# A planned transformer block on one core: the planner's durations are replaced by measured ones, and its settings and random draws are chosen again

## The chip, the cores and the metric

The kernel runs on one NeuronCore of a Trainium2 chip. The metric is the device time of one execution in microseconds (us). Five engines work side by side, each through its own instructions in a fixed order: PE (TensorE, matrix products), DVE (VectorE), ACT (ScalarE), POOL (GpSimd) and SP (SyncE, which here only issues transfers). They wait for each other through semaphores.

## The reference

One block of attention and one of an MLP, each behind a layer norm, over 2048 rows of 512 numbers, all in float32:

```python
h  = x + A(layernorm(x), wqkv, wo)
h2 = h + B(layernorm(h), w1, b1, w2, b2)

def A(x, wqkv, wo):          # 32 heads of 16; 8 keys a row, every second row back from it
    q, k, v = split(x @ wqkv)
    idx = pos[:, None] - 2 * arange(8)[None, :]
    logits = where(idx >= 0, einsum("hsd,hswd->hsw", q, k[idx]) * 16 ** -0.5, -1e9)
    return einsum("hsw,hswd->hsd", softmax(logits), v[idx]) @ wo

def B(x, w1, b1, w2, b2):    # 512 -> 1792 -> 512
    return relu(x @ w1 + b1) ** 2 @ w2 + b2
```

## The kernel before

**Products.** Every operand of a product is split into a high and a low part of a rounded float32 type (`hi` on ACT is a cast, `lo` on POOL or DVE a subtraction), and a product runs in three passes on PE: high by high, high by low and low by high. A pass over 128 rows and 512 columns is four matmuls of 512 columns.

**Groups.** The 2048 rows are worked in four groups of 512 (`u` = 0 to 3 in the code, four tiles of 128 rows each). For all groups x is normed, turned on PE and multiplied by `wqkv` (`qkv_first`, `qkv`); y goes to memory (`qkv_d`). The attention of a group is four items (`item`, one for 8 heads, so 16 in all). An item loads k, q and v; ACT copies q to PSUM (`qp`); DVE forms two products `pr<-qp,k` and sums them (`le<-pr`), does the softmax in small steps (ACT does the exponential, `le<-le`), forms two products `pr<-le,v`; POOL adds each of these up in three steps (`pr<-pr` of 1024, `pr<-pr` of 512, `o<-pr` of 256 numbers a row). There are three `pr` buffers.

**From attention to MLP** (`to_mlp`). For group 0 PE turns o (`tr<-ident,o`). For the other groups o is written to memory (`o_d<-o`, four times), read back in another order (`back<-o_d`), turned in blocks on DVE (`turned<-back`) and split by `split_turned`, whose operands have a stride: ACT casts `oh<-turned`, POOL subtracts `ol<-turned,oh`. Then PE multiplies by wo (`wo<-`), DVE adds h (`h<-wo,h`), and h is normed. For group 0 that is BN_STATS and BN_AGGR on DVE, three small operations on POOL (`rs`), the norm on ACT (`hn<-h,rs`) and a turn on PE (`tr<-ident,hn`). For the others it is four passes and a norm on ACT (`norm_act`), a way through memory (`t_d`, `back<-t_d`), `turned<-back` on DVE and the strided cast `big_h<-turned`. The result lies in `big_h` and `big_l`, in the place of the previous group's, so the casts wait until PE has read that for the last time.

**MLP.** For each of 14 blocks f of 128 hidden columns: PE multiplies by w1 (`mm<-`; for the first six blocks the weights are `w1a_h` and `w1a_l`, so the first matmul of a group's MLP reads `mm<-big_h,w1a_h`), ACT does the ReLU and the square (`r`, L742 and L744), ACT casts `rh<-r`, POOL subtracts `rl<-r,rh`, and PE adds the product with w2 to four sums (`acc<-w2s,rh` twice, `acc<-w2s,rl` once). The last group does pairs of blocks by a Winograd scheme (`win_pair`, `win_weights`, `win_rows`). w2 is split once (`w2_job`), kept in memory (`w_d`) and loaded again for every group (`w2s<-w_d`).

**What sets the order.** The code first records all work as tasks with a duration on each engine that may do it (`plan.add`); then `deadlines` gives each a due time, counted back from PE's place, with a random part (`NOISE`, `SEEDS`: one seed for each 40 us), and `schedule` places them one after another: on each engine the task that can start first, among equals the one due first. Some tasks may go to POOL or DVE, and the planner decides (`lo`, `add_any`). The instructions are then written out in the planned order; so the durations decide only about order and engine, and the chip waits where the order doesn't fit.

Durations come from `dv(n)` (DVE), `ac(n)` (ACT), `po(n)` (POOL) for n numbers a row, from numbers in the calls, and from `dma_us`. Settings are `BEFORE` (how much earlier the items of each group are due), `W2_EACH` (distance of the due times of `w2_job`), `LEAD` (how much earlier PE's turns rank), `NOISE` and `SEEDS`.

Of the kernel before, what the change touches and what calls it, by code (L numbers as in the profile page):

```python
# [15 lines left out]
S, D, H, DH, W, F = 2048, 512, 32, 16, 8, 1792  # L16
# [16 lines left out]
FA = 6  # L33
WARM = 46
ITEM = 16.0
BEFORE = 8, 16, 4, 16
X_BY_DRAM = (14, 15)
W2_EACH = 4.5
LO = ("POOL",)
LAGW = 2  # L40
NOISE, SEEDS = 0.3, (
    487, 765, 735, 246, 644, 701, 83, 442, 213, 893, 112, 220, 567, 914)
WIN = (0, 1, 2, 3, 4, 5, 6)
LEAD = 6.0
BY_PE = (0,)
TO_MLP = 10
T0 = 8.0
# [192 lines left out]


def dv(n):
    return (n + 157) / 960 + 0.01


def ac(n):
# [1 line left out]


def po(n):  # L250
    return 0.25 + 0.00214 * n


def dma_us(count, packet):
# [4 lines left out]
def block_kernel(ctx, tc, x, wqkv, wo, w1, b1, w2, b2, out):  # L259
    nc = tc.nc  # L260
# [47 lines left out]
    plan = Plan(bufs)  # L308
# [11 lines left out]
    def act(n, fn, extra=0.0, **k):  # L320
        return plan.add({"ACT": ac(n) + extra}, lambda e: fn(), **k)

    def vec(n, fn, **k):
        return plan.add({"DVE": dv(n)}, lambda e: fn(), **k)

    def pool(us, fn, **k):
        return plan.add({"POOL": us}, lambda e: fn(), **k)
# [2 lines left out]
        return plan.add({"SP": 0.45 if plan.pe < T0 + 1 else 0.55}, lambda e: fn(nc.sync),  # L330
                        dma=dma_us(count, packet), **k)

    def hi(n, dst, src, r, w, **k):
        act(n, lambda: nc.scalar.copy(dst(), src()), r=r, w=w, **k)  # L334

    def lo(n, dst, src, h, r, w, engs=("POOL", "DVE"), port=True, **k):
        cost = {"POOL": po(n), "DVE": dv(n)}
        plan.add({e: cost[e] for e in engs},
                 lambda e: engines[e].tensor_tensor(out=dst(), in0=src(), in1=h(),  # L339
                                                    op=ALU.subtract), r=r, w=w, port=port, **k)  # L340
# [18 lines left out]
    def norm_vec(src, dst, delay):  # L359
        st, mv, rs = (buf(n, (P, k)) for n, k in (("st", 6), ("mv", 2), ("rs", 2)))  # L360
        plan.add({"DVE": 0.70}, lambda e: nc.vector.bn_stats(st.get(), src.get()), r=[src], w=[st])
        plan.add({"DVE": 0.20}, lambda e: nc.vector.bn_aggr(mv.get(), st.get()), r=[st], w=[mv])

        def scale(e):
            m, s = mv.get(), rs.get()
            nc.gpsimd.tensor_scalar(out=s[:, 1:2], in0=m[:, 1:2], scalar1=EPS, scalar2=None,
                                    op0=ALU.add)
            nc.gpsimd.tensor_tensor(out=s[:, 0:1], in0=s[:, 1:2], in1=mhalf, op=ALU.pow)
            if delay:
                nc.gpsimd.tensor_scalar(out=s[:, 1:2], in0=m[:, 0:1], scalar1=s[:, 0:1],  # L370
                                        scalar2=-1.0, op0=ALU.mult, op1=ALU.mult)
        plan.add({"POOL": 1.15 if delay else 0.85}, scale, r=[mv, "mhalf"], w=[rs])
        if delay:
            act(D, lambda: nc.scalar.activation(blocked(dst, True), natural(src, True), AF.Identity,
                                                scale=rs.get()[:, 0:1], bias=rs.get()[:, 1:2]),
                0.2, r=[src, rs], w=[dst])
        else:

            plan.add({"DVE": 0.57}, lambda e: nc.vector.tensor_scalar(
                out=dst.get(), in0=src.get(), scalar1=mv.get()[:, 0:1], scalar2=None,  # L380
                op0=ALU.subtract), r=[src, mv], w=[dst])
        return rs

    def norm_act(src, dst, cls, by_pe):

        sq, sv = row("sq", cls), buf("sv", (P, 4))

        def sums(e):
            s = sv.get()
            nc.scalar.activation(sq.get(), src.get(), AF.Copy, accum_out=s[:, 0:1])  # L390
            nc.scalar.activation(s[:, 1:2], s[:, 0:1], AF.Copy, scale=-1.0 / D)
            nc.scalar.activation(sq.get(), src.get(), AF.Square, bias=s[:, 1:2],
                                 accum_out=s[:, 2:3])
            nc.scalar.activation(s[:, 3:4], s[:, 2:3], AF.Copy, scale=1.0 / D, bias=EPS)  # L394
        plan.add({"ACT": 2.2}, sums, r=[src], w=[sv, sq])
        pool(0.6, lambda: nc.gpsimd.tensor_tensor(out=sv.get()[:, 0:1], in0=sv.get()[:, 3:4],  # L396
                                                  in1=mhalf, op=ALU.pow), r=["mhalf"], w=[sv])

        def apply(e):
            s = sv.get()  # L400
            nc.scalar.activation(s[:, 2:3], s[:, 1:2], AF.Copy, scale=s[:, 0:1])
            nc.scalar.activation(blocked(dst, by_pe), natural(src, by_pe), AF.Identity, scale=s[:, 0:1],
                                 bias=s[:, 2:3])
        plan.add({"ACT": 1.1}, apply, r=[src, sv], w=[dst, sv])


    def pe_turn(srcs, r, **k):
# [49 lines left out]

    def split_turned(t, name):
        h, l = [row(name + p, CLASS[name], (P, KB, P), F32R) for p in "hl"]
        hi(D, lambda: by_block(h.get()), lambda: by_row(t), r=[t], w=[h])  # L460
        lo(D, lambda: by_block(l.get()), lambda: by_row(t), lambda: by_block(h.get()),
           r=[t, h], w=[l], engs=LO)
        return h, l

    def mm(n, ps, terms, width, start, stop, r, **k):
# [97 lines left out]
    def item(u, g, due, o):  # L563
        b, e = divmod(u, 2)
        src = lambda c: [("S", c, g, t) for v in ((u, u - 2) if b else (u,))
                         for t in range(v * R, v * R + R)] + ["zero"]
# [4 lines left out]
        def win(c, dst):  # L571
# [7 lines left out]
            r=src(0), w=[q], by=due - 8)  # L579
# [5 lines left out]
        for n, i0 in enumerate((0, IQ)):  # L585
# [5 lines left out]
                r=[qp, ks], w=[pr], by=due + 5 * n)  # L591
# [3 lines left out]
                r=[pr], w=[(LE, i0)], by=due + 5 * n + 1)  # L595
        if u < 2:
            tt("DVE", 256, lg, lg, lambda: mask.unsqueeze(3).to_broadcast([P, R, W, GH]), ALU.add,
               r=["mask"], w=lgs, by=due + 6)
        mx, sm = buf("mx", (P, R, GH)), buf("sm", (P, R, GH))
        vec(300, lambda: nc.vector.tensor_reduce(  # L600
            out=mx.get(), in_=lg().rearrange("p i w h -> p i h w"), axis=X, op=ALU.max),
            r=lgs, w=[mx], by=due + 6)
        tt("DVE", 256, lg, lg, lambda: mx.get().unsqueeze(2).to_broadcast([P, R, W, GH]),
# [1 line left out]
        act(256, lambda: nc.scalar.activation(LE.get()[:, 1], LE.get()[:, 0], AF.Exp,  # L605
                                             scale=DH ** -0.5),
            r=lgs, w=[exs], by=due + 6)
        vec(300, lambda: nc.vector.tensor_reduce(
            out=sm.get(), in_=ex().rearrange("p i w h -> p i h w"), axis=X, op=ALU.add),
            r=[exs], w=[sm], by=due + 8)  # L610
        vec(64, lambda: nc.vector.reciprocal(sm.get(), sm.get()), w=[sm], by=due + 8)
        tt("DVE", 256, ex, ex, lambda: sm.get().unsqueeze(2).to_broadcast([P, R, W, GH]),
           ALU.mult, r=[sm], w=[exs], by=due + 8)
        own = o is None
# [66 lines left out]
    def wo_product(t, oh, ol, h, pe, **k):  # L681
        ps = buf("ps", (P, D), name="wo")
        mm3(ps, ps.get, D, oh, ol, (lambda k: wo_h[:, k, :], [("wo", 0, k) for k in range(KB)]),
            (lambda k: wo_l[:, k, :], [("wo", 1, k) for k in range(KB)]), **k)
        tt("DVE", D, h.get, ps.get, h.get, ALU.add, r=[ps], w=[h], by=k["first"] + 3)
        hn = row("hn", "B")
        if pe:
            norm_vec(h, hn, True)
        else:
            norm_act(h, hn, "B", False)  # L690
        i = t % R
        if pe:
            ht = pe_turn([block(hn, k) for k in range(KB)], [hn])
        else:
            ht = turned(hn, "B")
        keys = [B(p, range(KB), [i]) for p in range(2)]

        def parts():
            if pe:
                view, src = lambda p: hh(p)[:, :, i, :], ht.get  # L700
            else:
                view, src = lambda p: by_block(hh(p)[:, :, i, :]), lambda: by_row(ht)
            hi(D, lambda: view(0), src, r=[ht], w=keys[0])
            lo(D, lambda: view(1), src, lambda: view(0), r=[ht] + keys[0],
               w=keys[1], engs=("DVE",) if pe else ("POOL", "DVE"), port=not pe)
# [47 lines left out]
    TT = [buf("pr", (P, 4, D), F32R, "tt") for _ in range(2)]  # L753

    def add_any(n, out_, a, b, op, **k):
        plan.add({"POOL": po(n), "DVE": dv(n)},
                 lambda e: engines[e].tensor_tensor(out=out_(), in0=a(), in1=b(), op=op),
                 port=True, **k)

# [176 lines left out]
    def consts():  # L936
# [1 line left out]
        nc.gpsimd.memset(mask, 0.0)  # L938
        nc.gpsimd.affine_select(out=mask, in_=mask, pattern=[[1, R], [1, W]], base=1 - W,
                                channel_multiplier=R, compare_op=ALU.is_ge, fill=NEG)  # L940
    pool(0.6, consts, w=["zero_sb", "mask"], by=0.0)
    load(192, 512, lambda q: q.dma_start(
        chain(0, 0, 0, 0, [[GC, PAD], [CS, 6 * G], [1, GC]]),
        zero.unsqueeze(1).to_broadcast([PAD, 6 * G, GC])), r=["zero_sb"],
# [207 lines left out]
```

## Time and profile before

| | us |
|---|---|
| median of 3 runs (lowest, highest) | 520.13 (519.19, 520.32) |
| the profiled execution, its own time | 520.07 |
| its span in the profile | 518.3 |
| PE busy | 502.3 |
| DVE busy | 369.3 |
| POOL busy | 334.0 |
| ACT busy | 302.1 |

The profile is one execution. A row of the timeline names the start, the length, the engine, the line, the operation and the tiles as out<-in; in brackets stands how long the engine had been idle before it, and what ended that. Matmuls overlap: a row of four matmuls of 512 columns lasts 1.07 us, but the next starts 0.91 us after it began. Idle time of an engine is a loss only where the end hangs on it.

### The profile page before, as it was taken

Reading aid. Unit: us, or ns where it says so; the run is one execution under the profiler, and the core shown is the slowest. Engines: PE = TensorE matmul, PEld = TensorE weight load, DVE = VectorE, ACT = ScalarE, POOL = GpSimd, SP = SyncE. Lnnn points to the kernel's source line nnn. Section 1 sums busy time; section 2 is a strip of 40 time slices with the busy share of each in tenths; the row PEclk is TensorE's granted clock in tenths of the full one; section 3 lists DMA queues with packets and bytes.
Section 4 is the critical chain, followed back from the end, with each engine's and each line's share of the span. In section 5 each row is a group of like instructions: output and inputs, shape, how many; then the busy total and the mean of one; then the engine's idle time right before and its main releaser. Section 6 shows DMA issues by size and latency. Waiting matters only on the chain.

```text
span 518.3 us, 7193 instructions
## 1 busy us (share of the span) xinstructions
PE 502.3 (97%) x2426; PEld 423.8 (82%) x2426; DVE 369.3 (71%) x406; ACT 302.1 (58%) x582; POOL 334.0 (64%) x282
## 2 busy tenths in 40 slices
PE   8999999999997999899989999999999999999997
PEld 8998888888876887687778888778887887988885
DVE  6379989989869877996774889988012486765633
ACT  4549868686254532579653467755356956574341
POOL 6102888784879697699889468679835132378920
PEclk9999999999998999999999999999999999999999
DMA  8699599999979975968784865934462856799842
GB/s 255 185 306 281 199 291 324 367 408 395 335 270 311 335 259 153 352 211 287 255 310 148 301 230 196 345 130 163 162 225 83 243 190 211 268 312 345 278 144 81
DMA packets 90229, 131.43 MB, mean 254 GB/s; under 512 B 7504, under 2 KB 57168, under 8 KB 90192
## 3 DMA queue, kind: packets, MB, share of 16 engines
q1 hardware_dynamic: 90048, 130.84, 75.2%
q8 instruction: 19, 0.31, 0.3%
q14 instruction: 18, 0.15, 0.1%
q10 hardware_dynamic: 144, 0.13, 0.1%
HBM read 93.63 MB, written 37.36 MB: 253 GB/s over the span
## 4 chain that ended last, share of the span: by engine, by line
PE 40%; POOL 11%; issue 6%; ACT 5%; DMA 5%; DVE 5%; SPq 1%; POOLq 0%; ACTq 0%; DVEq 0%
PE acc L880 17%; PE mm L469 11%; PE mm L840 6%; PE wo L469 4%; POOL pr L637 4%; DMA raw<-in_B_w_dram 2%; DVE pr L587 2%; ACT big_h L334 2%; DMA back<-o_d 2%; DMA back<-t_d 1%; POOL rl L339 1%; POOL o L637 1%; POOL ol L339 1%; POOL w2s L339 1%; DVE le L592 1%
## 5 line engine op out<-in xcount | busy, mean ns | idle before, releaser
L637 POOL TENSOR_TENSOR pr<-pr 128x1024 f32<-128x1024 f32 (+1 forms) x64 | 117.4, 1848 | 7.3 <-DVE pr L619 6.8
L880 PE MATMUL acc<-w2s,rh 128*128 128x512 f32 x444 | 111.4, 390 | 1.7 <-ACT rh L334 1.7
L339 POOL TENSOR_TENSOR rl<-r,rh 128x512 fp32r<-128x512 f32 x48 | 63.2, 1317 | 60.8 <-ACT rh L334 50.4
L880 PEld LDWEIGHTS acc<-w2s,rh 128*128 128x128 f32 x444 | 82.5, 188 | 19.1 <-ACT rh L334 2.5
L587 DVE TENSOR_TENSOR pr<-qp,k 128x2048 f32<-128x2048 f32 x32 | 72.6, 2278 | 17.1 <-POOL o L637 13.1
L619 DVE TENSOR_TENSOR pr<-le,v 128x2048 f32<-128x2048 f32 x32 | 72.6, 2285 | 11.6 <-POOL o L637 11.0
L592 DVE TENSOR_REDUCE le<-pr 128x128 f32<-128x2048 f32 x32 | 72.9, 2278 | 0.6
L742 ACT ACTIVATE r<-mm,b_sb 128x512 f32<-128x512 f32 x42 | 28.8, 686 | 72.0 <-PE mm L469 68.3
L880 PE MATMUL acc<-w2s,rl 128*128 128x512 f32 x222 | 60.5, 390 | 0.0
L469 PE MATMUL mm<-big_h,xh 128*128 128x512 f32 (+1 forms) x208 | 49.5, 376 | 0.3 <-ACT xh L334 0.3
L469 PE MATMUL mm<-big_h,xl 128*128 128x512 f32 (+1 forms) x208 | 49.7, 375 | 0.0
L469 PE MATMUL mm<-big_l,xh 128*128 128x512 f32 (+1 forms) x208 | 49.0, 374 | 0.0
L880 PEld LDWEIGHTS acc<-w2s,rl 128*128 128x128 f32 x222 | 41.0, 188 | 7.9
L469 PEld LDWEIGHTS mm<-big_h,xh 128*128 128x128 f32 x208 | 37.7, 188 | 6.3 <-ACT xh L334 1.1
L469 PEld LDWEIGHTS mm<-big_l,xh 128*128 128x128 f32 x208 | 38.1, 188 | 5.6
L469 PEld LDWEIGHTS mm<-big_h,xl 128*128 128x128 f32 x208 | 37.9, 188 | 5.4
L440 DVE STREAM_TRANSPOSE turned<-back 128x512 f32<-128x512 f32 x26 | 17.7, 696 | 28.9 <-DMA back<-o_d 19.6
L334 ACT CAST rh<-r 128x512 fp32r<-128x512 f32 x56 | 34.5, 619 | 1.6
L546 ACT COPY y<-mm 128x512 f32<-128x512 f32 x36 | 20.7, 587 | 14.9 <-PE mm L469 9.6
L469 PE MATMUL mm<-big_h 128*128 128x512 f32 x96 | 25.9, 394 | 2.1 <-ACT r L742 2.1
L744 ACT ACTIVATE r<-r 128x512 f32<-128x512 f32 x42 | 26.6, 634 | 1.0
L396 POOL TENSOR_TENSOR sv<-sv,mhalf 128x1 f32<-128x1 f32 x24 | 13.1, 549 | 21.7 <-ACT sv L394 21.6
(157 smaller groups left out, 956.6 us busy)
## 6 DMA issues: line engine op xcount, KB each, us to landing
w2s<-w_d SPq DMA_DIRECT2D x56, 512.0 KB, 4.7
k<-qkv_d SPq DMA_DIRECT2D x16, 704.0 KB, 5.5
v<-qkv_d SPq DMA_DIRECT2D x16, 704.0 KB, 4.9
raw<-in_B_w_dram SPq DMA_DIRECT2D x42, 256.0 KB, 6.6
qkv_d<-y SPq DMA_DIRECT2D x18, 512.0 KB, 6.6
w_d<-w2s SPq DMA_DIRECT2D x14, 512.0 KB, 6.5
xt<-in_A_x_dram SPq DMA_DIRECT2D x16, 256.0 KB, 4.3
q<-qkv_d SPq DMA_DIRECT2D x16, 256.0 KB, 6.6
```

Of the source, the lines that this page charges most:

```text
L334: act(n, lambda: nc.scalar.copy(dst(), src()), r=r, w=w, **k)
L339: lambda e: engines[e].tensor_tensor(out=dst(), in0=src(), in1=h(), op=ALU.subtract), r=r, w=w, port=port, **k)
L469: nc.tensor.matmul(ps(), l(), rr(), start=start and i == 0, stop=stop and i == len(terms) - 1)
L546: act(D, lambda: nc.scalar.copy(y.get()[:, :, j, :], ps.get().rearrange("p (j c) -> p j c", c=GC)), r=[ps], w=[(y, j)], by=plan.pe + 3)
L587: vec(2048, lambda pr=pr, i0=i0: nc.vector.tensor_tensor(out=pr.get(), in0=qp.get()[:, i0:i0 + IQ].unsqueeze(2).to_broadcast([P, IQ, W, GC ...
L592: vec(2048, lambda pr=pr, i0=i0: nc.vector.tensor_reduce(out=lg()[:, i0:i0 + IQ].rearrange("p i w h -> p (i w h)"), in_=pr.get().rearrange ...
L619: vec(2048, lambda p2=p2, i0=i0: nc.vector.tensor_tensor(out=p2.get(), in1=window(vs.get(), i0, [DH, GH], [1, DH]), op=ALU.mult, in0=ex()[ ...
L637: nc.gpsimd.tensor_tensor(out=dst, in0=a, in1=b_, op=ALU.add)
L742: act(D, lambda: nc.scalar.activation(r.get(), ps.get(), AF.Relu, bias=b1_sb[:, f:f + 1]), 0.08, r=[ps, "b1"], w=[r], keep=2)
L744: act(D, lambda: nc.scalar.activation(r.get(), r.get(), AF.Square), w=[r])
L840: nc.tensor.matmul(out_, win_w(pa, p, a)[:, kk], win_b(pb, j, kk), start=m + kk == 0, stop=m + kk == len(terms))
L880: nc.tensor.matmul(acc[j].get(), l.get()[:, j * P:(j + 1) * P], w2s.get()[:, wn], start=lead and n < len(js), stop=end and n >= len(terms) ...
```

## The change

It replaces durations of the planner: strided operations of turned tiles get more (ACT `oh` and `xh` by 0.5 us, `big_h` by 0.5, POOL's subtractions by 0.28, DVE's by 0.4), the norm's last step on ACT goes from 1.1 to 1.6 (or 1.2), POOL's small norm step from 1.15 to 1.4, unstrided work on DVE and POOL gets 0.02 to 0.05 us less, and a few small ones are set anew. Five settings and all 14 seeds are changed. No operation is added or left out, and none has another size; the order is another throughout, and 8 subtractions or additions that DVE did before are now POOL's (DVE 406 to 397 instructions, POOL 282 to 290; one plain copy is ACT's).

```diff
-BEFORE = 8, 16, 4, 16
+BEFORE = 8, 16, 4, 8
-W2_EACH = 4.5
+W2_EACH = 5.5
-NOISE, SEEDS = 0.3, (
-    487, 765, 735, 246, 644, 701, 83, 442, 213, 893, 112, 220, 567, 914)
+NOISE, SEEDS = 0.5, (
+    851, 120, 829, 921, 411, 801, 192, 673, 235, 703, 208, 492, 567, 710)
-LEAD = 6.0
+LEAD = 10.0
...
 def dv(n):
-    return (n + 157) / 960 + 0.01
+    return (n + 138) / 960 + 0.01
...
 def po(n):
-    return 0.25 + 0.00214 * n
+    return 0.2 + 0.00214 * n
...
-        cost = {"POOL": po(n), "DVE": dv(n)}
+        cost = {"POOL": po(n) + 0.7 * extra, "DVE": dv(n) + extra}
...
-        plan.add({"POOL": 1.15 if delay else 0.85}, scale, r=[mv, "mhalf"], w=[rs])
+        plan.add({"POOL": 1.4 if delay else 1.1}, scale, r=[mv, "mhalf"], w=[rs])
...
-        plan.add({"ACT": 1.1}, apply, r=[src, sv], w=[dst, sv])
+        plan.add({"ACT": 1.2 if by_pe else 1.6}, apply, r=[src, sv], w=[dst, sv])
...
-        hi(D, lambda: by_block(h.get()), lambda: by_row(t), r=[t], w=[h])
+        hi(D, lambda: by_block(h.get()), lambda: by_row(t), r=[t], w=[h], extra=0.5)
         lo(D, lambda: by_block(l.get()), lambda: by_row(t), lambda: by_block(h.get()),
-           r=[t, h], w=[l], engs=LO)
+           r=[t, h], w=[l], engs=LO, extra=0.4)
...
+            more = 0.0 if pe else 0.4
-            hi(D, lambda: view(0), src, r=[ht], w=keys[0])
+            hi(D, lambda: view(0), src, r=[ht], w=keys[0], extra=1.25 * more)
...
-        plan.add({"POOL": po(n), "DVE": dv(n)},
+        plan.add({"POOL": po(n), "DVE": dv(n) + 0.2},
```

Three places of the order follow, in rows that name the line, the operation, the tiles and the shape; lines after the 700th stand one further in the code after the change.

**Place 1: group 0, between wo and the MLP.** On DVE, from the third tile's BN_STATS to the fourth tile's BN_AGGR, before:

```order
L361 BN_STATS st<-h 128x6
L592 TENSOR_REDUCE le<-pr 128x128
L587 TENSOR_TENSOR pr<-qp,k 128x2048
L362 BN_AGGR mv<-st 128x2
L592 TENSOR_REDUCE le<-pr 128x128
L619 TENSOR_TENSOR pr<-le,v 128x2048
L361 BN_STATS st<-h 128x6
L619 TENSOR_TENSOR pr<-le,v 128x2048
L362 BN_AGGR mv<-st 128x2
```

And after:

```order
L361 BN_STATS st<-h 128x6
L608 TENSOR_REDUCE sm<-le 128x32
L362 BN_AGGR mv<-st 128x2
L611 RECIPROCAL sm<-sm 128x32
L361 BN_STATS st<-h 128x6
L587 TENSOR_TENSOR pr<-qp,k 128x2048
L344 TENSOR_TENSOR le<-le,sm 128x256
L362 BN_AGGR mv<-st 128x2
```

Of five large operations of attention (2048 numbers) that stood in between, one is left. On PE, around the last turns of hn and the first matmul of the MLP (`mm<-big_h,w1a_h`), before:

```order
L469 MATMUL mm<-big_h,xh 128x512 x4
L469 MATMUL mm<-big_h,xl 128x512 x4
L469 MATMUL mm<-big_l,xh 128x512 x4
L413 MATMUL tr<-ident,hn 128x128 x4
L469 MATMUL mm<-big_h,xl 128x512 x4
L413 MATMUL tr<-ident,hn 128x128 x8
L469 MATMUL mm<-big_h,w1a_h 128x512 x8
```

And after:

```order
L413 MATMUL tr<-ident,hn 128x128 x4
L469 MATMUL mm<-big_h,xh 128x512 x4
L413 MATMUL tr<-ident,hn 128x128 x4
L469 MATMUL mm<-big_l,xh 128x512 x4
L413 MATMUL tr<-ident,hn 128x128 x4
L469 MATMUL mm<-big_h,xl 128x512 x4
L469 MATMUL mm<-big_h,w1a_h 128x512 x8
```

The last two turns stood directly ahead of the MLP; now they lie apart, with four matmuls of the remaining qkv product behind the last.

**Place 2: group 1, the end of its attention and its way to wo.** On POOL, from the two adds of 1024 numbers of the group's last item to its last `o<-pr`, before:

```order
L637 TENSOR_TENSOR pr<-pr 128x2x512 x2
L339 TENSOR_TENSOR rl<-r,rh 128x512
L637 TENSOR_TENSOR pr<-pr 128x2x256
L339 TENSOR_TENSOR big_l<-raw,big_h 128x512
L637 TENSOR_TENSOR pr<-pr 128x2x256
L637 TENSOR_TENSOR o<-pr 128x2x32x4
L339 TENSOR_TENSOR rl<-r,rh 128x512
L637 TENSOR_TENSOR o<-pr 128x2x32x4
```

And after:

```order
L637 TENSOR_TENSOR pr<-pr 128x2x512 x2
L637 TENSOR_TENSOR pr<-pr 128x2x256
L339 TENSOR_TENSOR rl<-r,rh 128x512
L637 TENSOR_TENSOR o<-pr 128x2x32x4
L339 TENSOR_TENSOR big_l<-raw,big_h 128x512
L637 TENSOR_TENSOR pr<-pr 128x2x256
L339 TENSOR_TENSOR rl<-r,rh 128x512
L637 TENSOR_TENSOR o<-pr 128x2x32x4
```

The first `o<-pr` now stands ahead of the subtraction `big_l<-raw,big_h` and of the second add of 512. On SP, from the load of k of a later item over the write `o_d<-o` to the read `back<-o_d`, before:

```order
L572 DMA k<-qkv_d 128x1408
L577 DMA q<-qkv_d 128x512
L730 DMA w2s<-w_d 128x1024
L649 DMA raw<-in_B_w_dram 128x4x128
L484 DMA h<-in_A_x_dram 128x512
L1027 DMA o_d<-o 128x4x128
L730 DMA w2s<-w_d 128x1024
L649 DMA raw<-in_B_w_dram 128x4x128
L484 DMA h<-in_A_x_dram 128x512
L572 DMA v<-qkv_d 128x1408
L577 DMA q<-qkv_d 128x512
L434 DMA back<-o_d 128x4x512
```

And after:

```order
L572 DMA k<-qkv_d 128x1408
L577 DMA q<-qkv_d 128x512
L649 DMA raw<-in_B_w_dram 128x4x128
L731 DMA w2s<-w_d 128x1024
L1028 DMA o_d<-o 128x4x128
L484 DMA h<-in_A_x_dram 128x512
L649 DMA raw<-in_B_w_dram 128x4x128
L572 DMA v<-qkv_d 128x1408
L731 DMA w2s<-w_d 128x1024
L577 DMA q<-qkv_d 128x512
L434 DMA back<-o_d 128x4x512
```

One load of h went behind the write; k, q, one `raw` and one `w2s` stay ahead of it, and a v and a q stay between it and the read.

**Place 3: group 2, from the last reads of the old big_h to the first matmul of the MLP.** On PE, before (`mm<-big_h,big_l` is the last that reads the old `big_h`, and `mm<-big_h,w1a_h` the first that reads the new one):

```order
L469 MATMUL mm<-big_h 128x512 x4
L880 MATMUL acc<-w2s,rh 128x512 x8
L469 MATMUL mm<-big_h,big_l 128x512 x4
L880 MATMUL acc<-w2s,rl 128x512 x4
L469 MATMUL mm<-big_l,big_h 128x512 x4
L880 MATMUL acc<-w2s,rh 128x512 x8
L469 MATMUL mm<-big_h,w1a_h 128x512 x4
```

And after:

```order
L881 MATMUL acc<-w2s,rl 128x512 x4
L469 MATMUL mm<-big_h,big_l 128x512 x4
L881 MATMUL acc<-w2s,rh 128x512 x8
L469 MATMUL mm<-big_l,big_h 128x512 x4
L881 MATMUL acc<-w2s,rl 128x512 x4
L881 MATMUL acc<-w2s,rh 128x512 x8
L469 MATMUL mm<-big_h,w1a_h 128x512 x4
```

Eight matmuls of the w2 product have gone from ahead of the last read to behind it.

More of the change, by code (lines that the diff above doesn't have):

```diff
@@ L331, in load, with hi, lo @@
                         dma=dma_us(count, packet), **k)
-    def hi(n, dst, src, r, w, **k):
-        act(n, lambda: nc.scalar.copy(dst(), src()), r=r, w=w, **k)
-    def lo(n, dst, src, h, r, w, engs=("POOL", "DVE"), port=True, **k):
-        cost = {"POOL": po(n), "DVE": dv(n)}
+    def hi(n, dst, src, r, w, extra=0.0, **k):
+        act(n, lambda: nc.scalar.copy(dst(), src()), extra, r=r, w=w, **k)
+    def lo(n, dst, src, h, r, w, engs=("POOL", "DVE"), port=True, extra=0.0, **k):
+        cost = {"POOL": po(n) + 0.7 * extra, "DVE": dv(n) + extra}
         plan.add({e: cost[e] for e in engs},
@@ L599, in item @@
         mx, sm = buf("mx", (P, R, GH)), buf("sm", (P, R, GH))
-        vec(300, lambda: nc.vector.tensor_reduce(
+        vec(256, lambda: nc.vector.tensor_reduce(
             out=mx.get(), in_=lg().rearrange("p i w h -> p i h w"), axis=X, op=ALU.max),
@@ L607, in item @@
             r=lgs, w=[exs], by=due + 6)
-        vec(300, lambda: nc.vector.tensor_reduce(
+        vec(256, lambda: nc.vector.tensor_reduce(
             out=sm.get(), in_=ex().rearrange("p i w h -> p i h w"), axis=X, op=ALU.add),
             r=[exs], w=[sm], by=due + 8)
-        vec(64, lambda: nc.vector.reciprocal(sm.get(), sm.get()), w=[sm], by=due + 8)
+        vec(176, lambda: nc.vector.reciprocal(sm.get(), sm.get()), w=[sm], by=due + 8)
         tt("DVE", 256, ex, ex, lambda: sm.get().unsqueeze(2).to_broadcast([P, R, W, GH]),
@@ L702, in parts @@
                 view, src = lambda p: by_block(hh(p)[:, :, i, :]), lambda: by_row(ht)
-            hi(D, lambda: view(0), src, r=[ht], w=keys[0])
+            more = 0.0 if pe else 0.4
+            hi(D, lambda: view(0), src, r=[ht], w=keys[0], extra=1.25 * more)
             lo(D, lambda: view(1), src, lambda: view(0), r=[ht] + keys[0],
-               w=keys[1], engs=("DVE",) if pe else ("POOL", "DVE"), port=not pe)
+               w=keys[1], extra=more, engs=("DVE",) if pe else ("POOL", "DVE"), port=not pe)
         to_split.append(parts)
@@ L940, in consts @@
                                 channel_multiplier=R, compare_op=ALU.is_ge, fill=NEG)
-    pool(0.6, consts, w=["zero_sb", "mask"], by=0.0)
+    pool(1.5, consts, w=["zero_sb", "mask"], by=0.0)
     load(192, 512, lambda q: q.dma_start(
```

## The prediction

> **What bounds the kernel now.** I read the page's first part, then PE's waits, then PE's timeline at the longest of them, then the chain that ended last.
>
> ```profile
> PE 502.3 (97%) x2426; PEld 423.8 (82%) x2426; DVE 369.3 (71%) x406; ACT 302.1 (58%) x582; POOL 334.0 (64%) x282
> ...
> PE mm L469 <- ACT big_h L334: 4.2, 3, 1.8
> PE mm L469 <- ACT r L742: 2.1, 2, 1.1
> PE acc L880 <- ACT rh L334: 1.7, 2, 1.4
> PE tr L948 <- POOL ident masks.py:199: 1.3, 1, 1.3
> PE tr L413 <- ACT hn L374: 1.1, 1, 1.1
> PE wo L469 <- ACT oh L334: 0.8, 1, 0.8
> PE mm L840 <- ACT m L850: 0.7, 2, 0.4
> PE mm L469 <- ACT xh L334: 0.3, 1, 0.3
> ```
>
> PE is busy 97% of the span, and the change neither adds nor removes a matmul. So what an order can win is what PE waits: 12.2 us in the rows (total, times, longest), of which 1.3 is the start. Eight of these waits (all but the start and the four under 0.4) make nearly all of it. To each I add 0.16 us, since a matmul after a wait starts that much later than its place in the pipeline would be. About 12 us stand to be won, and one thing more:
>
> ```profile
> 162.82 0.75 PE L413 MATMUL tr<-ident,hn 128*128 128x128 f32 x4 [1.08 <-ACT hn L374]
> 165.09 3.45 PE L469 MATMUL mm<-big_h,w1a_h 128*128 128x512 f32 x8 [1.51 <-ACT big_h L334]
> ...
> 160.00:180.00 20.00, 17.40 (x74) 14.12 (x74) 18.90 (x19) 10.23 (x19) 14.73 (x14) 0.91 0.98 322
> ...
> 344.21 1.98 PE L880 MATMUL acc<-w2s,rh 128*128 128x512 f32 x8
> ```
>
> Eight matmuls last 1.98 us as a rule, and 3.45 right after the two waits of group 0. In that stretch of 20 us the granted clock (third number from the end) is 0.91. So these two waits cost 1.08 + 1.51 + 2 x 0.16 + 1.47 = 4.4 us.
>
> Where PE's waits come from is in the chain (start, length, what):
>
> ```profile
> 186.84 1.13 POOL pr L637
> ...
> 197.29 2.30 DVE pr L587
> ...
> 201.12 6.61 DMA raw<-in_B_w_dram
> ...
> 208.28 0.59 ACT qp L580
> ...
> 209.30 8.69 DMA back<-o_d
> ...
> 218.83 1.12 ACT oh L334
> ...
> 219.99 1.20 PE wo L469 x4
> ```
>
> From 187 to 219 us no matmul is in it. The attention of group 1 is late, and wo of that group waits for it. The waits of PE before 220 us (group 0's 4.4, r at 200, rh at 214, oh at 220, xh) lie beside this chain: had PE not lost them, it would have stood at wo earlier and waited there. So the 4.4 us are worth nothing by themselves; what group 1's attention gains is. That is the point on which the sum turns.
>
> **The change part by part.** First, are the new durations nearer? Forms, with the mean of one in ns:
>
> ```profile
> L334 ACT CAST oh<-turned 128x512 fp32r<-128x512 f32 x12 | 12.9, 1128 | 7.2 <-POOL ol L339 3.9 <-DVE turned L440 3.3
> L334 ACT CAST rh<-r 128x512 fp32r<-128x512 f32 x56 | 34.5, 619 | 1.6
> L339 POOL TENSOR_TENSOR ol<-turned,oh 128x512 fp32r<-128x512 f32 x12 | 18.7, 1568 | 6.5 <-ACT oh L334 6.3
> L339 POOL TENSOR_TENSOR rl<-r,rh 128x512 fp32r<-128x512 f32 x48 | 63.2, 1317 | 60.8 <-ACT rh L334 50.4 <-PE mm L469 7.4 <-PE acc L880 2.8
> L637 POOL TENSOR_TENSOR pr<-pr 128x512 f32<-128x512 f32 x32 | 41.0, 1292 | 0.4
> ```
>
> The old order took the strided cast for 0.61 us, as the plain one, and the strided subtraction for 1.35; the new one takes 1.11 and 1.58. They are right now, and four of a kind stand in a row at each group's change: 2 us that the old plan left out just where PE waits for `oh` and `big_h`. Since no instruction changes, durations alone cost nothing; all is in the order.
>
> Place 1, group 0. On DVE:
>
> ```profile
> 134.33 0.68 DVE L344 TENSOR_TENSOR h<-wo,h 128x512 f32<-128x512 f32 x1
> ...
> 149.90 2.29 DVE L587 TENSOR_TENSOR pr<-qp,k 128x2048 f32<-128x2048 f32 x1 [3.87 <-POOL o L637]
> ...
> 159.55 0.17 DVE L362 BATCH_NORM_AGGREGATE mv<-st 128x2 f32<-128x6 f32 x1
> ...
> 182.10 0.42 DVE L608 TENSOR_REDUCE sm<-le 128x32 f32<-128x256 f32 x1 [2.49 <-ACT le L605]
> ```
>
> The last tile's BN_AGGR came 25 us behind its `h<-wo`. In the new order one product of 2.29 and 14 small operations of at most 0.7 stand between them, 12 us at most. That is 13 us earlier, while by the order PE has about 25 us of matmuls between the group's last wo and the last turn of hn, before 28: 3 us less cover against a norm that comes 13 us earlier, so both waits end. The last turn has four matmuls (0.91 us) behind it before the MLP, and the turn's cast on ACT needs about 0.6 with its hand-over on both sides: 0.3 us stays. PE is then 4.1 us ahead here.
>
> Place 2, group 1. PE could start wo at 219.99 less its waits before that: 4.4 for group 0; 1.07 + 0.16 for r, 1.41 + 0.16 for rh, 0.77 + 0.16 for oh; 0.5 for xh: 8.7, so at 211.3, since as many matmuls stand ahead of wo as before. The attention's side: DVE has the same work ahead of the last product of item 8 (by the forms' means 164.1 us, before 163.5). It waited 3.87 for `o` and 2.49 for the exponential `le` in these 45 us. `le` stands on ACT behind the fourth `rh`, which comes from a matmul that is now 4.1 us earlier, so I count 2.5 less; the 3.87 I leave (POOL's work around it is as long as before). On POOL one add of 512 (1.29) and one subtraction (that of the 1.32 kind) have gone behind the first `o` of item 8; that frees the buffer on which the product at 197.29 waited, 2.6 earlier. From there the chain is unchanged: k is issued when that product ends, `raw` behind it (6.61), ACT's `qp` behind the cast of that `raw`, q on SP behind `qp`, and `back` behind q. The write of o went one load of h forward, which saves nothing as `back` isn't held by it. So `oh` comes 2.6 + 2.5 = 5.1 us earlier, 6.4 if a third of the 3.87 goes too. I take 6.5 for the start of wo, at 213.5; the ends are 2.6 (only POOL's step counts) and 8.7 (PE has no wait).
>
> Behind it: the waits of PE that remain, and the casts of group 2:
>
> ```profile
> 243.27 1.20 PE L469 MATMUL mm<-big_h 128*128 128x512 f32 x4 [1.00 <-ACT r L742]
> ...
> 260.74 1.20 PE L469 MATMUL mm<-big_h,w1a_h 128*128 128x512 f32 x4 [1.76 <-ACT big_h L334]
> ...
> 341.49 1.07 PE L469 MATMUL mm<-big_h,big_l 128*128 128x512 f32 x4
> 342.39 1.07 PE L880 MATMUL acc<-w2s,rl 128*128 128x512 f32 x4
> ...
> 347.13 1.20 PE L469 MATMUL mm<-big_h,w1a_h 128*128 128x512 f32 x4 [0.95 <-ACT big_h L334]
> ...
> 342.59 3.03 ACT L334 CAST big_h<-turned 128x512 fp32r<-128x512 f32 x3 [1.55 <-PE mm L469]
> ```
>
> At 260.74 group 1's last `big_h` was late. The last wo matmul of the group now stands 27.6 us of matmuls ahead of the MLP, before 23.9, and DVE has 13 us of work between its last `h<-wo` and the last `turned`, before 15. With 3.7 + 1.4 us more against a wait of 1.92 it goes: -1.9.
>
> At 347.13 (place 3) the casts begin when PE has read the old `big_h` for the last time (342.39) and need until 347.1: 4.7 us. Behind that read stood 16 matmuls, 3.64 us; now there are 24, 5.45: -1.1. At 243.27 r stands on ACT behind the norm as before, but the two blocks of the MLP that PE did there in one go are now mixed with w2 products: half goes, -0.6 (ends 0 and -1.2). The small waits in the Winograd part I leave; some of its differences and four strided subtractions are POOL's now instead of DVE's, and PE's first products are reordered for that: 0, between -1.5 (all its waits) and +1.5 (one strided subtraction of 1.57 too late).
>
> What is late next:
>
> ```profile
> 302.57 1.09 PE L469 MATMUL wo<-wo_h,oh 128*128 128x512 f32 x4
> ...
> 301.31 1.09 ACT L334 CAST oh<-turned 128x512 fp32r<-128x512 f32 x1
> ...
> 387.18 1.07 PE L469 MATMUL wo<-wo_h,oh 128*128 128x512 f32 x4
> 385.72 2.97 ACT L334 CAST oh<-turned 128x512 fp32r<-128x512 f32 x3
> ```
>
> In groups 2 and 3 `oh` is ready 0.2 to 0.5 us ahead of wo: a PE that comes earlier waits there. It would reach group 2's wo at 302.57 - 6.5 - 0.6 - 1.9 + 0.9 (wo stands four matmuls later) = 294.5, and `oh`, 6.5 earlier as group 1's, is there at 295.9: +1.4, between 0 and 3.5. In group 3 DVE has 2.3 us less ahead of the last product, so I count 0 there.
>
> Sum against the execution's own 520.07: -6.5 - 0.6 - 1.9 - 1.1 + 0 + 1.4 = -8.7, 511.4. The median of the runs, 520.13, is 0.06 above it, so I predict 511.5. The ends taken together: -8.7 - 1.2 - 1.9 - 1.1 - 1.5 gives 505.7, and -4.9 - 1.9 + 2 + 1.5 gives 516.8; as they hardly meet, its own range is 507 to 515.
>
> **The rivals.** (a) Attention still decides at group 1: `le` or `o` hold DVE as before and wo starts at 219.99. Then the later terms alone count, -0.6 - 1.9 - 1.1, with +1.4 at group 2: 517.9. For it speaks the chain without a matmul and the same 164 us of DVE work; against it the two steps on POOL. (b) No change: as (a), and the 8.7 us of PE's waits come together at group 1's wo. A stretch of idle of more than 2.6 us was followed by eight slow matmuls at 165.09, so 1.5 us come on top: 519.4. The Trainium skill, TensorE: Matmul & The Clock Gate, Part 1, says that PE's clock falls to half after an idle window of about 3.4 us and needs as long at work to come back; by that rule the loss would be 1.7 us. The trace agrees with it at 165 us and has no single wait long enough to test it. (c) Slower: group 3's items are due 8 us later against the other work (`BEFORE` from 16 to 8). If its attention ends 8 us later, `oh` comes at 394.8 instead of 386.8 and wo at 395.2 instead of 387.18: 528. It decides from the point where group 3's `oh` comes over 1 us later than now. Against it speaks that as much PE work stands ahead of group 3's wo, and 2 us more POOL work and 2 us less DVE work ahead of its last item.
>
> **How the numbers follow.** The forecast 0.60; (a) 0.22; (b) 0.07; (c) 0.11. Faster is the forecast and (a), 0.82; within 0.2% (1.04 us, about what a measurement of this kernel can tell) is (b), 0.07; slower (c), 0.11. The range takes in the forecast's own and (a) with half a microsecond: 507.0 to 518.5, which leaves out (b), (c) and a few in a hundred below.
>
> **What would show it.** Right: no wait at hn, and a granted clock of 1.00 in all stretches of 20 us but the last; wo of group 1 between 211 and 215 us with `oh` as releaser or none; no wait over 0.3 us at the first `w1a_h` of groups 1 and 2; group 2's wo with a wait of 1 to 2 us for `oh`. Wrong: group 1's wo at 218 or later, with DVE's waits for `o` and `le` as before it; a wait for `oh` of over 3 us in group 2 or 3; POOL's subtractions as releasers of PE in the Winograd part.

## The result, and the profile after

The changed kernel takes 513.08 us (median of 6 runs, 511.2 to 514.26) against 519.27 us for the kernel before beside it (6 runs, 518.58 to 520.32). The ratio is 0.9877, with an interval of 0.9853 to 0.9901: 6.2 us faster. The profiled execution took 512.46 us, with a span of 510.7 against 518.3. Forecast were 511.5 us and a range of 507.0 to 518.5.

PE's busy time, and all that it waits for (total us, times, longest), in the profile after:

```profile
PE 501.4 (98%) x2426; PEld 424.4 (83%) x2426; DVE 361.7 (71%) x397; ACT 303.4 (59%) x583; POOL 343.6 (67%) x290
```

```profile
PE tr L413 <- DVE xl L339: 2.0, 1, 2.0
PE tr L949 <- POOL ident masks.py:199: 1.3, 1, 1.3
PE mm L841 <- ACT m L851: 1.2, 2, 1.0
PE wo L469 <- ACT oh L334: 0.6, 1, 0.6
PE wo L469 <- ACT r L743: 0.2, 1, 0.2
```

PE waits 5.3 us instead of 12.2. No wait for `hn`, `big_h` or `rh` is left. But 2.0 us are new, a wait for `xl`, in a stretch of the kernel where there was none before. PE's timeline at the marks of the prediction (start, length; in brackets the wait):

```profile
57.51 1.10 PE L413 MATMUL tr<-ident,xn 128*128 128x128 f32 x4 [1.99 <-DVE xl L339]
58.26 2.05 PE L469 MATMUL mm<-big_h,xl 128*128 128x512 f32 x4
...
165.98 1.33 PE L469 MATMUL mm<-big_h,w1a_h 128*128 128x512 f32 x5
...
216.87 1.20 PE L469 MATMUL wo<-wo_h,oh 128*128 128x512 f32 x4 [0.64 <-ACT oh L334]
...
254.99 1.07 PE L469 MATMUL mm<-big_h,w1a_h 128*128 128x512 f32 x4
...
297.60 1.07 PE L469 MATMUL wo<-wo_h,oh 128*128 128x512 f32 x4
...
339.47 1.07 PE L469 MATMUL mm<-big_h,w1a_h 128*128 128x512 f32 x4
...
379.37 1.07 PE L469 MATMUL wo<-wo_h,oh 128*128 128x512 f32 x4
```

The MLP of group 0 starts without a wait, but not earlier than before (165.98, before 165.09): what was won there had been lost at 57.5, where a wait of 1.99 us and slow matmuls behind it (2.05 us for four) cost about 3 us. wo of group 1 starts 3.1 us earlier (219.99 before), the MLP of group 1 5.8, wo of group 2 5.0, the MLP of group 2 7.7, wo of group 3 7.8, and PE ends 7.6 us earlier.

Where the new wait comes from is on DVE:

```profile
47.08 2.28 DVE L619 TENSOR_TENSOR pr<-le,v 128x2048 f32<-128x2048 f32 x1
49.40 2.29 DVE L592 TENSOR_REDUCE le<-pr 128x128 f32<-128x2048 f32 x1
54.47 2.29 DVE L619 TENSOR_TENSOR pr<-le,v 128x2048 f32<-128x2048 f32 x1 [2.78 <-POOL o L637]
56.68 0.68 DVE L339 TENSOR_TENSOR xl<-tr,xh 128x512 fp32r<-128x512 f32 x1
```

The second product of an item waits 2.78 us for POOL's `o`, and `xl` stands behind it on DVE. `o` is the last reader of the item's *first* product. In the program as built, the library under the kernel has given both products the same one of the three `pr` buffers, though another was free: its last reader is the sum at 49.40, which ends at 51.69. (The run `after_pr` below shows it: with another buffer the wait is gone.) The planner counts on the buffer that comes free first. The kernel asks for a tile of a tag with three buffers, and the library chooses. The same happens in group 1:

```profile
194.81 2.29 DVE L587 TENSOR_TENSOR pr<-qp,k 128x2048 f32<-128x2048 f32 x1 [3.06 <-POOL o L637]
```

Another buffer was free at 191.75 here. This product is the last reader of the k on whose buffer SP's next load waits, and so `back<-o_d` and `oh`. SP's queue shows it: k is issued when the product ends, and the read stands behind it:

```profile
197.13 0.32 SPq L572 DMA_DIRECT2D k<-qkv_d  x1
...
206.14 0.38 SPq L434 DMA_DIRECT2D back<-o_d  x1
```

In the kernel before, the products at 149.90 (3.87) and 197.29 (4.86) waited in the same way. The prediction had read these waits as a matter of POOL's order.

### The profile page after: what moved, and what is told of

It reads as the page before. It is cut to its first block, busy times and chain, and to the rows that moved or that the text cites. A ratio compares the mean times of both kernels' runs of the same rounds, so it can differ in the third digit from the quotient of the medians.

```text
span 510.7 us, 7199 instructions
## 1 busy us (share of the span) xinstructions
PE 501.4 (98%) x2426; PEld 424.4 (83%) x2426; DVE 361.7 (71%) x397; ACT 303.4 (59%) x583; POOL 343.6 (67%) x290
## 4 chain that ended last, share of the span: by engine, by line
PE 85%; DVE 7%; POOL 3%; issue 2%; ACT 2%; POOLq 0%; DVEq 0%; ACTq 0%
PE mm L469 41%; PE acc L881 25%; PE wo L469 9%; PE mm L841 7%; POOL pr L637 2%; DVE pr L619 2%; PE tr L413 2%; DVE le L592 2%; DVE pr L587 2%; PE tr L949 1%; POOL o L637 1%; ACT oh L334 0%; DVE r L344 0%; PE half L1111 0%; POOL rl L339 0%
## 5 line engine op out<-in xcount | busy, mean ns | idle before, releaser
L339 POOL TENSOR_TENSOR rl<-r,rh 128x512 fp32r<-128x512 f32 x43 | 56.1, 1308 | 37.3 <-ACT rh L334 37.0
L469 PE MATMUL mm<-big_h,xl 128*128 128x512 f32 (+1 forms) x208 | 51.3, 381 | 0.0
L469 PE MATMUL mm<-big_l,xh 128*128 128x512 f32 (+1 forms) x208 | 50.1, 375 | 0.0
```

The lines of the kernel that those rows point to most:

```text
L469: nc.tensor.matmul(ps(), l(), rr(), start=start and i == 0, stop=stop and i == len(terms) - 1)
```

## The experiments

Ratios are to the kernel before, run on the same chip, with their intervals. Some of the runs were made on different chips; where two such runs are compared, the difference of the ratios stands beside that of the medians.

**Do PE's waits add up, or does attention decide?** The kernel before, with the norm of group 0 moved ahead by hand, as the new order has it: tasks of the finished plan are put right behind other ones (946, 957 and 958 are the BN_AGGR of the third tile and both of the fourth, 935, 947 and 959 the steps on POOL, 936, 948 and 960 `hn`).

```diff
+    by_n = {t.n: t for t in plan.order}
+    for tn, tm in [(946, 945), (957, 946), (958, 957), (935, 406), (947, 935),
+                   (959, 947), (936, 935), (948, 947), (960, 959)]:
+        tk = by_n[tn]
+        plan.order.remove(tk)
+        at = plan.order.index(by_n[tm]) + 1
...
+        plan.order.insert(at, tk)
     for t in plan.order:
         t.fn(t.on)
```

> The kernel before with one part of the new order done by hand: in group 0 the last two tiles' BN_STATS and BN_AGGR stand ahead of attention's products on DVE, their three small operations on POOL and the norms hn on ACT right behind those of the second tile. PE's waits at hn and big_h with the slow matmuls behind them (4.4 us) should go. Theory A (group 1's attention sets its wo): the MLP of group 0 starts 3 to 4 us earlier, wo of group 1 still at 220 us, no gain: 519.3 us within 0.7. Theory B (PE's waits add up): 514.9 us.

519.27 us, ratio 1.0008 (0.9999 to 1.0016). The wait for `hn` went, but the last cast of `big_h` stood behind `le` on ACT, and PE waited there:

```profile
166.11 2.12 PE L469 MATMUL mm<-big_h,w1a_h 128*128 128x512 f32 x8 [2.82 <-ACT big_h L334]
```

So this run tells nothing apart: PE had not been made earlier. The mended one leaves the steps of the second and third tile on POOL where they were, and moves `le` (445) behind the last cast:

```diff
-    for tn, tm in [(946, 945), (957, 946), (958, 957), (935, 406), (947, 935),
-                   (959, 947), (936, 935), (948, 947), (960, 959)]:
+    for tn, tm in [(946, 945), (957, 946), (958, 957), (959, 947), (948, 947),
+                   (960, 959), (445, 972)]:
```

> The kernel before with one part of the new order done by hand, mended: in group 0 the last two tiles' BN_STATS and BN_AGGR stand ahead of attention's products on DVE, the fourth tile's three small operations on POOL and its norm hn on ACT right behind the third's, and the last cast of big_h stands ahead of the exponential le on ACT, behind which it had come in the first attempt (wait of 2.82 us at 166.11). PE's waits at hn and big_h with the slow matmuls (4.4 us) should go, with the MLP of group 0 starting 3 to 4 us earlier. Theory A (the chain of attention through DVE and POOL sets wo of group 1, and PE's waits of group 0 don't hold it): wo of group 1 within 1 us of 220, 519.0 us within 0.7. Theory B (PE's waits add up): wo of group 1 at 216, 514.9 us.

518.31 us, ratio 0.9984 (0.9972 to 0.9995): 0.65 us by the medians. PE's timeline, and ACT's at the second row:

```profile
163.36 2.14 PE L469 MATMUL mm<-big_h,w1a_h 128*128 128x512 f32 x8 [0.75 <-ACT big_h L334]
...
200.38 1.19 PE L469 MATMUL mm<-big_h 128*128 128x512 f32 x4 [3.20 <-ACT r L742]
...
218.80 1.19 PE L469 MATMUL wo<-wo_h,oh 128*128 128x512 f32 x4 [0.84 <-ACT oh L334]
```

```profile
199.12 0.59 ACT L580 COPY qp<-q 128x512 f32<-128x512 f32 x1 [6.46 <-DVE pr L587]
199.64 0.68 ACT L742 ACTIVATE r<-mm,b_sb 128x512 f32<-128x512 f32 x1
```

The wait at 162.8 is gone and 0.75 us is left at the MLP. PE waits for `r` at 200 instead, 3.20 us where it was 1.07, since `r` stands on ACT behind `qp`, which waits for attention's product on DVE. wo moves by 1.2 us of the 3.5 that were taken away, 0.2 more than theory A allowed, and the time by 0.65 where theory B had 4.4. Theory A holds in the main: attention decides at group 1, and it reaches PE through ACT's queue as well as through `oh`.

Now the new wait of PE taken away from the changed kernel, `xl` (227) moved ahead of the waiting product (274), a swap of two neighbours on DVE:

```diff
+    for tn, tm in [(274, 227)]:
```

> The changed kernel with one edit: on DVE the subtraction xl<-tr,xh, behind which PE waited 2.0 us at 57.5 us, stands ahead of the product pr<-le,v that waits there for POOL's o. PE's wait and its slow matmuls behind it (together 3.1 us) should go. Theory A (group 1's attention sets the start of its wo): PE then stands at that wo at about 213 us and waits there until oh comes at 216.8 as before; no gain, 513.1 us within 0.5. Theory B (PE's waits add up): wo starts 3 us earlier and the time is 510.0 us.

510.48 us, ratio 0.9838 (0.9825 to 0.985): 2.6 us less than the changed kernel's 513.08, or 2.0 by the ratios. Theory A as I had put it is wrong here, and theory B's numbers came out (wo 3 us earlier, 510.0):

```profile
213.27 1.19 PE L469 MATMUL wo<-wo_h,oh 128*128 128x512 f32 x4 [1.40 <-ACT oh L334]
```

`oh` itself came 3.6 us earlier. 0.8 of that was there from the first product on, which waits for its load of k, and 0.5 is the swap's own, since DVE now does this `xl` while it would wait for `o`. The main reason is in DVE's queue (changed kernel first, then this one):

```profile
61.98 0.69 DVE L339 TENSOR_TENSOR xl<-tr,xh 128x512 fp32r<-128x512 f32 x1 [1.02 <-ACT xh L334]
```

```profile
59.52 0.68 DVE L339 TENSOR_TENSOR xl<-tr,xh 128x512 fp32r<-128x512 f32 x1
```

The next `xl`, which needs a turn by the late PE, made DVE wait 1.02 us (and the one behind it 0.38), and with it attention. So while qkv runs, PE and attention hold each other up through `xl`. An early wait of PE counts where DVE waits for PE in turn, and not in group 0's norm, where it doesn't.

**The buffers.** The order is kept to the row; only the buffer of each `pr` tile is the one that the planner counted on. The last two lines shown are in `schedule`.

```diff
-        return Buf(tag, lambda: pool.tile(list(shape), dt, name=name or tag, tag=tag,
-                                          bufs=bufs[tag]))
+        def make():
+            if tag in ('pr',):
+                return pool.tile(list(shape), dt, name=name or tag, tag="%s%d" % (tag, b.slot), bufs=1)
...
+                if b.tag in ids:
+                    b.slot = min(ids[b.tag])[1]
```

> The changed kernel with the planner's order kept, but each pr tile put into the buffer that the planner counted on (three tags of one buffer each in place of one tag of three). In the trace after, two DVE products waited for the buffer of the tile before them while another of the three was free: pr at 54.47 us (free 2.77 us earlier) and pr at 194.81 us (free 3.06 us earlier). The first holds xl and so PE at 57.5 us, the second is the last reader of the k that SP loads at 197.1 us, in whose queue raw, q and the read back<-o_d of group 1 stand. Theory A (the attention of group 1 sets wo, and that buffer holds it): oh and wo come about 3 us earlier, at 213.8 us, and the time is 510.1 us, between 509 and 511.5. Theory B (something else in the chain, the load of raw or the write of o, is as late): wo at 216 to 217 us, 512.5 to 513.1 us.

> The kernel before with its order kept, and each pr tile in the buffer that the planner counted on. Two DVE products waited for the tile before them while another buffer was free: pr at 149.90 us (free 3.9 us earlier) and pr at 197.29 us (free 4.9 us earlier). Theory A (group 1's attention sets wo): wo starts at about 215 us instead of 219.99, and PE's own waits ahead of it decide by how much less: 514.5 us, between 512 and 516. Theory B (the waits for a buffer are hidden): 519.3 us within 0.5.

> The changed kernel in its own order, with every tile of every pool (not pr alone) in the buffer that the planner counted on. Theory A (only the pr buffers were given otherwise to any effect): 507.7 us within 0.7, as with pr alone. Theory B (other pools hold work up in the same way, such as kv, whose loads stand in SP's queue): over 1 us faster, under 506.7 us.

The changed kernel goes from 513.08 to 507.7 us (ratio 0.9791, 0.9778 to 0.9804), the kernel before to 512.87 (0.9886, 0.9868 to 0.9905). With all tiles so placed, not `pr` alone, the changed kernel takes 506.88 (0.9777, 0.9758 to 0.9795). That lies between what the two theories allowed, and the intervals overlap: whether other pools cost something is not settled, and it is below 1 us. The products in the changed kernel with its `pr` placed, and its PE:

```profile
51.51 2.29 DVE L629 TENSOR_TENSOR pr<-le,v 128x2048 f32<-128x2048 f32 x1
...
187.75 2.29 DVE L597 TENSOR_TENSOR pr<-qp,k 128x2048 f32<-128x2048 f32 x1
```

```profile
55.11 0.63 PE L423 MATMUL tr<-ident,xn 128*128 128x128 f32 x4
...
211.69 1.19 PE L479 MATMUL wo<-wo_h,oh 128*128 128x512 f32 x4 [0.28 <-ACT oh L344]
```

Both waits of DVE are gone, and PE's at 57.5 with them. wo starts 5.2 us earlier instead of the 3 that theory A counted, and the time is below its range of 509 to 511.5: both savings count, one by 57 us and one at 194. In the old order wo starts at 213.95, 6.0 us earlier and without a wait, and the time is within theory A's range. So the choice of buffers alone was worth 5.4 us in the new order (4.5 by the ratios) and 5.9 in the old, nearly as much as the whole change.

**Durations or settings and draws?** (Of the 14 seeds 13 differ; the last but one is 567 in both.)

The first two kernels take one half of the change each: the changed kernel with the five lines that follow, and the kernel before with these lines the other way round. The other two have the planner's `pr` buffers as well.

```diff
-BEFORE = 8, 16, 4, 8
+BEFORE = 8, 16, 4, 16
-W2_EACH = 5.5
+W2_EACH = 4.5
-NOISE, SEEDS = 0.5, (
-    851, 120, 829, 921, 411, 801, 192, 673, 235, 703, 208, 492, 567, 710)
+NOISE, SEEDS = 0.3, (
+    487, 765, 735, 246, 644, 701, 83, 442, 213, 893, 112, 220, 567, 914)
-LEAD = 10.0
+LEAD = 6.0
```

> The changed kernel with its new durations, but the settings (BEFORE, W2_EACH, LEAD), NOISE and SEEDS of before. Theory A (a time comes from how late the plan itself ends and from what the chip adds to it): the planner's own end is 518.2 us here, against 507.1 before and 505.5 after, and the chip's spans were 11.2 and 5.2 us above it; with the new durations' 5.2 that is a span of 523.4 and a time of 525 us, between 521 and 530, so slower than before. Theory B (truer durations alone give the better order): 513 us within 2.

> The kernel before with its old durations, but the new settings, NOISE and SEEDS. Theory A (plan's end plus what the chip adds): the planner's own end is 515.0 us, and with the old durations' 11.2 above it the span is 526.2 and the time 528 us, between 523 and 532. Theory B (the settings and draws are the gain, the durations don't matter): 513 us within 2.

> As dur_only, and each pr tile in the buffer that the planner counted on. With these buffers the chip's span was 0.3 us above the planner's end for the new durations and order (505.8 against 505.5) and 3.1 above it for the old (510.2 against 507.1). Theory A (the new durations make the plan true, the buffers were the rest): span 518.2 + 0.3, time 520.3 us, within 1.5. Theory B (0.3 was luck of that one order): over 522 us.

> Old durations, new settings and draws, and each pr tile in the buffer that the planner counted on. The planner's own end is 515.0 us. Theory A (with these buffers the chip adds what the durations have wrong: 3.1 us above the plan for the old durations in the order of before, 0.3 and 1.4 for the new ones in two orders): span 518.1, time 519.9 us, between 518 and 522. Theory B (the durations' errors are of no weight, the buffers alone were): span within 1.4 of 515.0, time 517 to 518 us.

Each half alone is slower than before: the durations 522.43 us (1.0064, 1.0041 to 1.0086), the settings and draws 522.03 (1.0053, 1.0034 to 1.0072). That holds with the planner's buffers too: 520.62 (1.0038, 1.0015 to 1.0061) and 521.9 (1.0066, 1.0044 to 1.0087), where the old order with these buffers takes 512.87. So neither half is the gain. The draws go with the durations beside which they stand: with the one or the other exchanged, the planner's own end is 8 to 13 us later. The settings were not parted from the draws. PE's longest wait with the new settings and draws on the old durations:

```profile
258.72 2.50 PE L469 MATMUL mm<-big_h,w1a_h 128*128 128x512 f32 x5 [5.55 <-ACT big_h L334]
```

Of these 5.55 us the planner has 3.2 in its own plan.

The planner's own end (what its code returns) against the spans of the profiles, in us:

| durations | settings and draws | planner's end | span, library's `pr` | above | span, planner's `pr` | above |
|---|---|---|---|---|---|---|
| old | old (before) | 507.1 | 518.3 | 11.2 | 510.2 | 3.1 |
| old | new | 515.0 | 518.7 | 3.7 | 519.1 | 4.1 |
| new | old | 518.2 | 522.2 | 4.0 | 519.6 | 1.4 |
| new | new (changed) | 505.5 | 510.7 | 5.2 | 505.8 | 0.3 |
| new | four other seeds | 505.0 | 506.9 | 1.9 | 503.2 | -1.8 |

Each span is of one execution, and the executions of one kernel differ by up to 5 us, so the medians have to bear the reading too (a median less 1.8 us stands for a span). With the planner's buffers the old durations leave the chip 3 to 4 us behind the plan (two orders; 3.9 and 5.1 by the medians), the new ones -1.8 to 1.4 (three; -1.7 to 0.6). What the library's buffers add depends on the order: -0.4 to 8.1 us (0.1 to 5.9 by the medians). My expectation for set_only had carried the 11.2 over as if it belonged to the durations, and was 6 us too high.

So the difference of the two spans, 7.6 us, parts into three: the new plan ends 1.6 us earlier (507.1 to 505.5), it is kept better by 2.8 (3.1 to 0.3), and the buffers cost 4.9 instead of 8.1, 3.2 less. The medians shift the last two parts. With the planner's buffers, on one chip, the change takes 512.87 to 507.7: 5.2 us, of which 1.6 are the plan's end and 3.6 its being kept. The buffers then cost 5.4 (4.5 by the ratios) instead of 5.9, only 0.5 to 1.4 less, and the intervals of the ratios don't tell that from nothing. So most of the gain is the plan and its being kept; whatever the buffers gave was chance as far as the change goes, since no one of its numbers speaks of the choice of buffers.

**Does the chip now follow the plan with other draws?** Four seeds of the changed kernel are set anew, so that the planner's end is 0.55 us earlier.

```diff
-    851, 120, 829, 921, 411, 801, 192, 673, 235, 703, 208, 492, 567, 710)
+    851, 120, 513, 571, 411, 801, 192, 673, 235, 703, 129, 492, 783, 710)
```

> The changed kernel with four other seeds (the planner's own end is 505.0 us, 0.55 earlier than with the seeds of the change) and each pr tile in the buffer that the planner counted on; the order differs in about a quarter of the rows of every engine. Theory A (with true durations and buffers the chip follows the plan, whatever the draws): span 505.3 to 506.4, time 507.1 to 508.2 us. Theory B (the seeds of the change were lucky on the chip): over 509 us.

> The changed kernel with the four other seeds of the run before, but its pr tiles in one tag of three buffers, as in the kernels before and after. With the planner's own buffers this order took 505.1 us (span 503.2, planner's end 505.0), and no engine's wait held PE but the start. Theory A (the buffers that the library gives pr tiles hold DVE up, as in the changed kernel, where they cost 5.4 us): 508 to 513 us. Theory B (these seeds are better by themselves): 505.1 us within 1.

With the planner's `pr` buffers 505.12 us (0.9742, 0.9726 to 0.9759), the fastest of all: 8.0 us less than the changed kernel (7.0 by the ratios). All that PE waits for in it:

```profile
PE tr L959 <- POOL ident masks.py:199: 1.3, 1, 1.3
```

With the library's buffers it takes 510.37 us (0.9845, 0.9818 to 0.9872): DVE waits 2.77 us at 54.2 for the same buffer as in the changed kernel, and PE 2.00 us for `xl` again. So the buffers are worth 5.2 us in this order. The first run was 2 us better than theory A's range, the second within it; the lucky draw of theory B is refuted, by one other set of draws.

## Why the prediction was right, and which step was not

The sign and the mechanism were right: fewer waits of PE, with group 1's attention as the point that decides. The size was 8.6 us by the forecast and 6.2 by the medians. In one execution each, PE's end moved by 7.6. That this is near the forecast is luck in part: the first step fell short by 3.4, and the others gave 2.3 more than counted. Step by step:

- **wo of group 1, -6.5 forecast, -3.1 measured.** This is the step that failed. Its part on POOL held: 2.6 forecast for `o` ahead of two operations, and `o` and the product that waits for it came 2.5 earlier (197.29 to 194.81), from the same start of POOL's adds (before, then after):

```profile
186.80 4.77 POOL L637 TENSOR_TENSOR pr<-pr 128x1024 f32<-128x1024 f32 x2
...
196.52 0.74 POOL L637 TENSOR_TENSOR o<-pr 128x256 f32<-128x256 f32 x1
```

```profile
186.78 6.05 POOL L637 TENSOR_TENSOR pr<-pr 128x1024 f32<-128x1024 f32 x3
...
194.01 0.77 POOL L637 TENSOR_TENSOR o<-pr 128x256 f32<-128x256 f32 x1
```

  Its other part, 2.5 for `le` and a third of the 3.87 for `o`, was to bring DVE to the last product of item 8 3.8 us earlier. It got there 0.7 earlier (185.62 to 184.93), and POOL, busy with the item before until 186.8 in both, could make nothing of that. From 126 to 185 us DVE does wait 3.5 us instead of 9.0 (waits over 0.2 us). But from 30 to 126 us, where I hadn't looked since the work ahead was the same 164 us, it waits 8.9 instead of 5.3; new there are 2.78 at 54.47 and 2.07 at 76. Their cause, the buffer, is in no order, and a wait for `o` was in the trace of before to be asked about: which buffer, and which others were free? Behind the product 0.6 us more came, which I had put at nothing: most of it because `raw` is now issued ahead of a `w2s`, 1.0 us behind k instead of 1.5.
- **The MLP of group 1, -0.6 and -1.9.** From wo to the first `w1a_h` it was 40.75 us and is 38.12: -2.6. Both waits went; that for `r`, of which I had left a half, went wholly.
- **wo of group 2, +1.4.** There is no wait: 41.83 us and now 42.61, of which 0.9 is the four matmuls more. PE came 3.1 us later than forecast and `oh` 1.4 (297.3), so `oh` was in time.
- **The MLP of group 2, -1.1.** 44.56 us and now 41.87, less the same 0.9: -1.8. The wait for `rh` at 329.5, which I had not counted, went too.
- **The Winograd part, 0.** From wo of group 3 to the end it was 127.4 us and is 127.6. PE's waits for `m` are 1.2 instead of 0.7.
- **The range.** Its upper sum takes -4.9 for wo of group 1 and +2 for the wait of group 2, where the terms themselves end at -2.6 and +3.5, and it leaves out the -1.1 of the MLP of group 2: by the terms it is 519.5, not 516.8. PE's waits ahead of wo add up to 8.6, not 8.7.

Rival (a) was right by half: DVE reached the last product of item 8 hardly earlier, though through new waits, while POOL's step came. Rival (b)'s slow matmuls came, at 58 us and not at group 1's wo. Rival (c) did not come: group 3's `oh` was ready at 379.0, before at 386.8.

The sentence that the 4.4 us at group 0 are worth nothing by themselves held in the run that took 3.5 of them away. Two marks of being right were missed: wo of group 1 came at 216.87, not between 211 and 215, and group 2's wo has no wait. A granted clock of 1.00 everywhere (third number from the end) was missed too:

```profile
40.00:60.00 20.00, 18.01 (x85) 15.22 (x84) 16.08 (x13) 15.26 (x39) 9.72 (x9) 0.94 0.77 231
...
160.00:180.00 20.00, 20.00 (x95) 16.69 (x94) 19.51 (x20) 12.80 (x24) 15.76 (x12) 1.00 0.93 311
```

## What to carry to other kernels

Where a planner sets the order, compare its own end with the chip's span: the difference says how much is still in the planner's model, and a search over draws is worth only what the model keeps. Besides durations the model has to know who hands out the buffers; a wait for the last reader of one tile while another buffer stands free is the sign that it doesn't, and one tag for each buffer mends it. An engine's early wait counts if an engine on the deciding chain waits for it in its own queue, so ask in both directions before it is called hidden.

## What the runs showed of the hardware

Nearly the same wait of PE, in the same place, is followed by slow matmuls in one order and not in another (one execution of each). In the changed kernel 1.99 us of waiting at 57.5 were followed by four matmuls of 2.05 us (above). In the order with four other seeds and the library's buffers:

```profile
57.24 0.72 PE L413 MATMUL tr<-ident,xn 128*128 128x128 f32 x4 [2.00 <-DVE xl L339]
57.72 1.17 PE L469 MATMUL mm<-big_h,xl 128*128 128x512 f32 x4
```

After 2.82 and 3.20 us (the rows at 166.11 and 200.38 above) there were none; after 5.55 us there were (2.50 us for five, the granted clock 0.50 from 258 to 262 us). The changed kernel's six executions spread over 3.1 us, that of 511.2 us with a mean granted clock of 1.000 and that of 514.26 with 0.995, though one of 513.7 has 0.999, so the clock isn't all of it; the version in which PE has no wait but the start spreads over 0.26 us (four executions). The Trainium skill, TensorE: Matmul & The Clock Gate, Part 1, puts the fall at an idle window of about 3.4 us that runs free of the kernel's start. That the phase matters agrees with these rows; that 2.0 us can be enough does not. At 165 us in the kernel before, the forecast saw agreement; there is some in the loss (1.47 us against the estimate of 1.7 by that rule), none in the idle time: the two waits, 1.08 and 1.51 us, have four turns between them, and together they are 2.6 us.
